# Block products of Strassen type for gates and projection, and conversion of the weights in pieces of 1024 values

## The chip, the cores and the metric

The kernel runs on one core of one Trainium2 chip. Its engines each have a queue of their own: TensorE multiplies matrices (its weight loads are shown apart from its matmuls), VectorE and ScalarE work on tiles element by element, GpSimd does almost nothing here, and SyncE issues all the DMAs. TensorE writes its sums to PSUM; the other tiles lie in SBUF. The metric is the time of one execution on the device in microseconds, and the median of three runs is given.

## The reference

```python
kv = np.einsum('bhsd,bhse->bhde', k, v)          # b 8, h 8, s 576, d 64
out = np.einsum('bhsd,bhde->bhse', q, kv)
rms = np.sqrt(np.mean(out * out, axis=-1, keepdims=True) + 1e-06)
attn = out / rms * g_norm
x = attn.transpose(0, 2, 1, 3).reshape(4608, 512)
h = (x @ w1) * (x @ w2) @ w3                     # w1, w2 512x1024, w3 1024x1024
y = h @ w_out                                    # w_out 1024x512
```

The four weights come as 64-bit floats and are turned into 32-bit ones on the chip. The rest is 32-bit throughout.

## The kernel before

A batch has 576 rows. 512 of them form a group of their own (T = 0 to 7), and the 64 left over of each of the eight batches form the ninth (T = 8), so every group has 512 tokens. For a group the kernel keeps x transposed in `xT[T]` (128 partitions, 4 chunks of the 512 features, 512 tokens).

`gate(T, f)` (line 316) computes block f of 8: two accumulations of four matmuls, weights 128x128 against 512 tokens, one for w1 and one for w2, each in a PSUM bank; ScalarE copies the first to `a_sb`, VectorE multiplies it with the second into `ab[T, f]`. `project(T)` (373) multiplies these blocks with `w3o_sb`, the product of w3 and w_out, which is made once: four output tiles, each an accumulation of eight matmuls 512 wide, then a copy by ScalarE or VectorE and a store.

The stages follow one another. First attention of batch 0 runs. Then the gates of T = 0 run while weights arrive: `load_raw` (115) loads 512 values per partition into a ring of four tiles, and `convert` (121) turns them into 32-bit floats, with two operations on ScalarE and four on VectorE. Then comes the fold: for each of eight blocks of w3 it converts, turns it by TensorE (`turn_w3`, 344) and multiplies it with w_out (`fold_block`, 363). Attention of batch 1 is laid between the fold's blocks. Then follows `project(0)`, and for T = 1 to 8 the gates, with the pieces of attention(T + 1) laid between the blocks, the loads of batch T + 2, and the projection.

`attention(b)` (162) gives pieces for the two halves of the eight heads: `kv`, `q_t`, `product` with its `norm`, and `turn`, which writes `xT`. For odd b it also treats the rows left over of two batches (`q_t_left`, `product_left`, `turn_left`); there are then nine pieces for eight blocks, and the last two follow each other. A piece takes its PSUM banks from `ps_at` (three of them), gates, folds and projections from `ps_mm` (five).

The order on TensorE is that of the program. Up to the end of the gates of T = 0, so are the orders on VectorE, ScalarE and SyncE; from there on a planner orders them. The head of the program, with the order written out:

```python
for name in ("kv1", "q_t01", "q_t11", "turn00", "product01", "turn10"):
    first[name]()
convert_gates(0, raws[0][:1])
first["product11"]()
keep_warm(4)
for name in ("turn01", "turn11"):
    first[name]()
convert_gates(0, raws.pop(0)[1:])
```

## Time and profile before

| | us |
|---|---|
| median of three runs | 956.66 |
| lowest, highest | 955.62, 961.29 |
| the profiled execution | 959.86 |
| its span, first to last instruction | 958.0 |
| TensorE busy | 922.6 |
| VectorE busy | 221.9 |
| ScalarE busy | 189.7 |

The time of an execution holds a little more than the span of its instructions. PE is TensorE, PEld its weight load, DVE VectorE, ACT ScalarE, SPq the queue from which SyncE issues DMAs. A row of a group of instructions gives line, engine, operation, tile written and tiles read, shapes and count, then busy time, the mean duration of one in ns, and the idle time before them with what ended it. A row in order of time gives start, length and the same names; in brackets stands the idle time just before it and what released it. Matmuls overlap, so the length of a row of them is a little more than the time until the next may start; the pace is read from starts. A row of a stretch gives its length, the busy time of PE, PEld, DVE, ACT and POOL with the count of instructions, the clock granted to TensorE (1.00 is full), the busy share of the DMA engines and the GB/s moved.

### The profile page before, as it was taken

The page shows a single profiled execution, that of the slowest core. Times are in us where ns is not written, and L with a number is a line of the kernel's source. Part 1 is how long each engine was busy: PE and PEld are TensorE (multiplying, and loading weights), DVE is VectorE, ACT ScalarE, POOL GpSimd, SP SyncE. Part 2 cuts the span into 40 slices and gives each one's busy share as a digit, 9 for nine tenths or more (in the row PEclk, how much of TensorE's full clock was granted, in tenths as well). Part 3 has the DMA queues.
Part 4 walks back from the last instruction along what each step waited for, and adds up shares of the span by engine and source line. Part 5 has one row for each costly group of instructions (what it writes and reads, how often), then busy time and mean ns, then how long its engine had stood idle before and what let it go on. Part 6 is the DMA issues. An engine that isn't in the chain of part 4 may idle for free.

```text
span 958.0 us, 8045 instructions
## 1 busy us (share of the span) xinstructions
PE 922.6 (96%) x3280; PEld 459.6 (48%) x3280; DVE 221.9 (23%) x421; ACT 189.7 (20%) x364; POOL 0.7 (0%) x6
## 2 busy tenths in 40 slices
PE   7896799999999998999999989999999899999998
PEld 7342455445544554455445544554455444444443
DVE  3878873102110221021102120211021200100010
ACT  3545542102110221022102120221022200000000
POOL 0000000000000000000000000000000000000000
PEclk9898799999999999999999999999999899999999
DMA  8487733002201120022002201220000000000001
GB/s 236 155 267 250 239 99 83 12 33 72 72 11 58 48 72 22 34 72 72 12 34 71 72 12 44 72 61 22 33 1 1 1 36 8 1 22 23 0 1 44
DMA packets 55620, 59.24 MB, mean 62 GB/s; under 512 B 15136, under 2 KB 47904, under 8 KB 55584
## 3 DMA queue, kind: packets, MB, share of 16 engines
q1 hardware_dynamic: 55584, 58.73, 19.9%
q8 instruction: 26, 0.43, 0.2%
q14 instruction: 10, 0.08, 0.0%
HBM read 49.28 MB, written 9.44 MB: 61 GB/s over the span
## 4 chain that ended last, share of the span: by engine, by line
PE 88%; DMA 4%; DVE 3%; ACT 2%; issue 1%; SPq 1%; ACTq 0%; DVEq 0%
PE mm L321 46%; PE mm L378 26%; PE mm L367 6%; DMA raw<-in_moe_w_dram 3%; PE at L176 3%; PE at L239 3%; PE at L198 2%; PE at L271 1%; PE mm L350 1%; DMA v_sb<-in_v_dram 1%; DVE low L138 1%; ACT w_sb L131 1%; DVE inv L218 1%; DVE xn L226 0%; ACT low L130 0%
## 5 line engine op out<-in xcount | busy, mean ns | idle before, releaser
L321 PE MATMUL mm<-xT,w_sb 128*128 128x512 f32 x1024 | 449.9, 594 | 0.7 <-DVE w_sb L142 0.7
L321 PEld LDWEIGHTS mm<-xT,w_sb 128*128 128x128 f32 x1024 | 191.8, 191 | 226.7 <-issue 222.8
L378 PE MATMUL mm<-w3o_sb,ab 128*128 128x512 f32 x576 | 254.3, 603 | 0.0
L378 PEld LDWEIGHTS mm<-w3o_sb,ab 128*128 128x128 f32 x576 | 111.1, 194 | 138.0 <-issue 138.0
L332 DVE TENSOR_TENSOR ab<-a_sb,mm 128x512 f32<-128x512 f32 x72 | 49.5, 687 | 426.8 <-PE mm L321 426.8
L330 ACT COPY a_sb<-mm 128x512 f32<-128x512 f32 x72 | 42.1, 585 | 208.8 <-PE mm L321 208.8
L386 ACT COPY o_sb<-mm 128x512 f32<-128x512 f32 x18 | 10.6, 586 | 248.7 <-PE mm L378 248.7
L367 PE MATMUL mm<-wo_sb,w3T 128*128 128x512 f32 x128 | 56.8, 597 | 0.0
L388 DVE COPY o_sb<-mm 128x512 f32<-128x512 f32 x18 | 12.5, 692 | 184.9 <-PE mm L378 184.9
L321 PE MATMUL mm<-x_left,w_sb 128*128 128x512 f32 x128 | 55.1, 592 | 0.0
L216 ACT ACTIVATE sq<-at 128x512 f32<-128x512 f32 (+1 forms) x40 | 22.1, 552 | 92.1 <-PE at L239 91.0
L239 PEld LDWEIGHTS at<-kv_bd,qT 128*128 128x128 f32 x256 | 32.9, 192 | 12.8 <-issue 11.5
L321 PEld LDWEIGHTS mm<-x_left,w_sb 128*128 128x128 f32 x128 | 24.3, 190 | 30.6 <-issue 30.6
L367 PEld LDWEIGHTS mm<-wo_sb,w3T 128*128 128x128 f32 x128 | 24.0, 193 | 27.1 <-issue 27.1
L130 ACT ACTIVATE low<-raw 128x512 f32<-128x512 uint32 x40 | 27.1, 678 | 42.1 <-DMA raw<-in_moe_w_dram 26.6
L239 PE MATMUL at<-kv_bd,qT 128*128 128x128 f32 x256 | 33.8, 276 | 0.9 <-ACT qT L200 0.9
L218 DVE TENSOR_REDUCE inv<-sq 128x8 f32<-128x512 f32 (+1 forms) x40 | 25.3, 631 | 31.8 <-ACT sq L216 31.8
L275 ACT ACTIVATE xT<-at,g_col 128x512 f32<-128x512 f32 x32 | 21.9, 685 | 47.3 <-PE at L271 47.3
L200 ACT COPY qT<-at 128x512 f32<-128x512 f32 x32 | 18.5, 585 | 64.3 <-PE at L198 64.3
L138 DVE SCALAR_TENSOR_TENSOR low<-raw,low 128x512 uint32<-128x512 uint32 x40 | 27.3, 685 | 1.6 <-ACT low L130 1.5
L226 DVE TENSOR_TENSOR xn<-at,inv 128x512 f32<-128x512 f32 (+1 forms) x40 | 25.5, 638 | 4.0
L271 PE MATMUL at<-ident,xn 128*128 128x128 f32 x128 | 19.8, 278 | 5.3 <-DVE xn L226 4.8
(44 smaller groups left out, 314.5 us busy)
## 6 DMA issues: line engine op xcount, KB each, us to landing
raw<-in_moe_w_dram SPq DMA_DIRECT2D x32, 512.0 KB, 5.2
k_sb<-in_k_dram SPq DMA_DIRECT2D x16, 512.0 KB, 4.4
v_sb<-in_v_dram SPq DMA_DIRECT2D x16, 512.0 KB, 5.5
q_sb<-in_q_dram SPq DMA_DIRECT2D x16, 512.0 KB, 3.9
out_dram<-o_sb SPq DMA_DIRECT2D x32, 256.0 KB, 2.3
raw<-in_moe_w_out_dram SPq DMA_DIRECT2D x8, 512.0 KB, 5.0
kl_sb<-in_k_dram SPq DMA_DIRECT2D x16, 64.0 KB, 4.3
vl_sb<-in_v_dram SPq DMA_DIRECT2D x16, 64.0 KB, 4.8
```

What stands on the lines that cost most here:

```text
L130: nc.scalar.activation(low, lo, AF.Copy, scale=2.0 ** -51, bias=2.0)
L138: nc.vector.scalar_tensor_tensor(out=low_bits, in0=hi, scalar=0x80000000, in1=low_bits, op0=ALU.bitwise_and, op1=ALU.bitwise_or,)
L176: nc.tensor.matmul(kv_ps[e * D:(e + 1) * D, r, :], lhsT=k_sb[:, h, cols] if j < J else kl_sb[:, h, :], rhs=v_sb[:, h, cols] if j < J else ...
L218: nc.vector.tensor_reduce(out=inv, in_=sq[:, cols].rearrange("p (h d) -> p h d", d=D), axis=AX.X, op=ALU.add,)
L226: nc.vector.tensor_tensor(out=dst, in0=o_ps[:, cols].rearrange("p (n m d) -> p n m d", m=m, d=D), in1=inv.rearrange("p (n m) -> p n m", m= ...
L239: nc.tensor.matmul(o_ps[:, h * P:(h + 1) * P], lhsT=qT[i, half][:, h, :], rhs=bd[:, half * HB + h, :], start=True, stop=True,)
L271: nc.tensor.transpose(t_ps[:, r, j, :], st[i, half][:, j, 2 * r:2 * r + 2, :], ident)
L321: nc.tensor.matmul(g_ps, lhsT=w_sb[:, f, c, :], rhs=xT[T][:, c, :], start=(c == 0), stop=(c == NP - 1),)
L330: nc.scalar.copy(a_sb, prods[0])
L332: nc.vector.tensor_mul(ab[T, f], a_sb, prods[1])
L367: nc.tensor.matmul(f_ps, lhsT=t[:, j, :], rhs=wo_sb[:, j, :], start=(j == 0), stop=(j == KF - 1))
L378: nc.tensor.matmul(o_ps, lhsT=ab[T, f][:, m * P:(m + 1) * P], rhs=w3o_sb[:, f, :], start=(f == 0), stop=(f == KF - 1),)
```

## The change

Gates of T = 1 to 8 and all nine projections become products of 2x2 blocks by a scheme of Strassen type, with seven block products where eight stood (`winograd`). For the gates a pair of feature blocks, p and p + 4, is taken at once, the two halves of the 512 features are the inner blocks, and the two halves of the 512 tokens the columns; w1 and w2 go through it together, as the two halves of a PSUM bank. For the projection the inner blocks are pairs of `ab` and `w3o_sb`. Every matmul is now 256 columns wide.

A product goes into a bank; ScalarE copies that partial sum to SBUF (`keep`) while the bank stays as it is, and a later product is added onto it there. Three banks are used per call. VectorE adds a bank and a kept sum (`done`) and, in the gates, multiplies the two halves. The sums of blocks that the scheme needs are made by VectorE: of the weights once (`sum_w`), of `w3o_sb` once (`combine_w3o`), of `ab` for each pair and group (`sum_ab`), of x for each group (`combine_x`). Each writes three new tiles and one block in place.

The gates of T = 0 and the fold keep their matmuls. Weights are loaded and converted in pieces of 1024 values per partition, w1 and w2 of a block in one piece, through a ring of four such pieces, and each conversion issues the next load. The first conversion now follows the whole of attention of batch 0. The fold takes its blocks in the order 0, 4, 1, 5, 2, 6, 3, 7. The input tiles of a half batch have one buffer in place of two, so the second half is loaded after the first has been used, in the middle of a group's gates. The pieces for the rows left over come one place earlier, so that there are eight pieces always; a pair of blocks has two places for them (`between`). Tiles of the first stages are given back, and the sums take their room. A store of the projection holds two of the four output tiles.

```diff
+    N = G // 2
...
-    inp = ctx.enter_context(tc.tile_pool(name="inp", bufs=2))
-    fold = ctx.enter_context(tc.tile_pool(name="fold", bufs=2))
+    inp = ctx.enter_context(tc.tile_pool(name="inp", bufs=1))
...
+    conv = tc.tile_pool(name="conv", bufs=1)
+    early = tc.tile_pool(name="early", bufs=1)
...
+    w_sb = const.tile([P, KF, 2, NP, P], FP32, name="w_sb")
...
+    def load_raw(*srcs):
+        raw = conv_pool.tile([P, 1024], srcs[0].dtype, name="raw", bufs=RAW)
+        n = 1024 // len(srcs)
+        for i, src in enumerate(srcs):
+            nc.sync.dma_start(
+                out=raw[:, i * n:(i + 1) * n].rearrange("p (c m) -> p c m", c=src.shape[1]),
+                in_=src,
+            )
         return raw
...
+        words = raw.bitcast(U32).rearrange("p (n w) -> p n w", w=2)
+        lo, hi = words[:, :, 0], words[:, :, 1]
+        low = conv_pool.tile([P, 1024], FP32, name="low", bufs=2)
...
+    FOLD_ORDER = [i + h * NF for i in range(NF) for h in range(2)]
+    RAW = 4
+    todo = [("w", 0), ("w", 1), ("w", 2)]
+    for f in range(3, KF):
+        todo += [("w", f)] + [("w_out", f // 2 - 1)] * (f % 2)
+    todo += [("w3", i) for i in FOLD_ORDER]
+    todo.insert(-KF + 2, ("w_out", NF - 1))
...
+    raws = []
+    def load_next():
+        if len(raws) == len(todo):
+            return
+        what, i = todo[len(raws)]
...
+    converted = []
+    w3_sb = {}
+    def convert_next(what):
+        n = len(converted)
+        assert todo[n][0] == what
+        i = todo[n][1]
...
+        convert(dst, raws[n])
+        converted.append(n)
+        load_next()
...
-        x = xT[b] = work.tile([P, NP, G], FP32, name="xT")
+        x = xT[b] = work.tile([P, 2, 2, NP // 2, N], FP32, name="xT")
...
+            dst = x[:, half, i].rearrange("p r (j t) -> p r j t", j=2)
+            nc.scalar.activation(dst, t_ps, AF.Copy, scale=g_col)
...
         if b % 2:
-            pieces[6] += [(q_t_left,)]
-            pieces[7] += [(product_left,)]
-            pieces += [[(turn_left,)]]
+            pieces[5] += [(q_t_left,)]
+            pieces[6] += [(product_left,)]
+            pieces[7] += [(turn_left,)]
...
+    ab = [const.tile([P, 4, N], FP32, name=f"ab{p}") for p in range(NF)]
...
-        a_sb = work.tile([P, G], FP32, name="a_sb")
+        a_sb = conv_pool.tile([P, G], FP32, name="a_sb", bufs=2)
         nc.scalar.copy(a_sb, prods[0])
-        ab[T, f] = work.tile([P, G], FP32, name="ab", bufs=KF + 1)
-        nc.vector.tensor_mul(ab[T, f], a_sb, prods[1])
+        half = f // NF
+        nc.vector.tensor_mul(
+            ab[f % NF][:, 2 * half:2 * half + 2, :],
+            a_sb.rearrange("p (i t) -> p i t", i=2),
+            prods[1].rearrange("p (i t) -> p i t", i=2),
+        )
...
+    def winograd(lhsT, rhs, chunks, done, between=lambda: None):
+        def product(a_name, b_name, to=None):
+            ps = to if to is not None else bank(ps_mm, "mm").rearrange("p (u n) -> p u n", u=2)
+            for u in range(2):
+                for c in range(chunks):
+                    nc.tensor.matmul(
+                        ps[:, u, :],
+                        lhsT=lhsT(a_name, u, c),
+                        rhs=rhs(b_name, c),
+                        start=(u == 0 and c == 0 and to is None),
+                        stop=(c == chunks - 1),
+                        skip_group_check=True,
+                    )
+            return ps
+        def keep(name, ps):
+            t = late_pool.tile([P, 2, N], FP32, name=name)
+            nc.scalar.copy(t, ps)
+            return t
+        r1 = product("a11", "b11")
+        p1 = keep("p1", r1)
+        r2 = product("s1", "t1")
+        p5 = keep("p5", r2)
+        product("s2", "t2", r1)
+        u2 = keep("u2", r1)
+        between()
+        product("s4", "b22", r2)
+        done("c12", r2, u2)
+        product("s3", "t3", r1)
+        u3 = keep("u3", r1)
+        done("c22", p5, u3)
+        r3 = product("a12", "b21")
+        done("c11", r3, p1)
+        between()
+        product("a22", "t4", r1)
+        done("c21", r1, None)
+    def combine(b, free):
+        t = {"t1": free[0], "t2": free[1], "t3": b["b12"], "t4": free[2]}
+        args = [
+            (t["t1"], b["b12"], b["b11"]), (t["t2"], b["b22"], t["t1"]),
+            (t["t3"], b["b22"], b["b12"]), (t["t4"], b["b21"], t["t2"]),
+        ]
+        b.update(t)
+        return [lambda a=a: nc.vector.tensor_sub(*a) for a in args]
+    def sums(a, free):
+        s = {"s1": free[0], "s2": free[1], "s3": a["a21"], "s4": free[2]}
+        args = [
+            (s["s2"], s["s1"], a["a11"]), (s["s4"], a["a12"], s["s2"]), (s["s3"], a["a11"], a["a21"]),
+        ]
+        first = (s["s1"], a["a21"], a["a22"])
+        a.update(s)
+        return [lambda: nc.vector.tensor_add(*first)] + [
+            lambda a=a: nc.vector.tensor_sub(*a) for a in args
+        ]
+    def run(*step_lists):
+        for steps in zip(*step_lists):
+            for step in steps:
+                step()
+    xb, wa, aa, ob = {}, {}, {}, {}
+    free = {}
+    def allocate():
+        h = NP // 2
+        for p in range(NF):
+            free["w", p] = late_pool.tile([P, 3, 2, h, P], FP32, name=f"ws{p}")
+        for p in range(NF):
+            free["ab", p] = late_pool.tile([P, 3, N], FP32, name=f"as{p}")
+            free["w3o", p] = late_pool.tile([P, 3, N], FP32, name=f"os{p}")
+    def parts(t):
+        return [t[:, i] for i in range(3)]
+    def combine_x(T):
+        xb[T] = {f"b{i + 1}{j + 1}": xT[T][:, i, j] for i in range(2) for j in range(2)}
+        t = late_pool.tile([P, 3, NP // 2, N], FP32, name="xc")
+        return combine(xb[T], parts(t))
+    def sum_w(p):
+        h = NP // 2
+        wa[p] = {
+            f"a{i + 1}{j + 1}": w_sb[:, p + i * NF, :, j * h:(j + 1) * h]
+            for i in range(2) for j in range(2)
+        }
+        return sums(wa[p], parts(free["w", p]))
+    def sum_ab(p):
+        aa[p] = {name: ab[p][:, i, :] for i, name in enumerate(("a11", "a21", "a12", "a22"))}
+        return sums(aa[p], parts(free["ab", p]))
+    def combine_w3o(p):
+        ob[p] = {
+            f"b{i + 1}{j + 1}": w3o_sb[:, p + i * NF, j * N:(j + 1) * N]
+            for i in range(2) for j in range(2)
+        }
+        return combine(ob[p], parts(free["w3o", p]))
+    AB_OF = {"c11": 0, "c12": 1, "c21": 2, "c22": 3}
+    def gates(T, p, between):
+        def done(name, one, two):
+            dst = ab[p][:, AB_OF[name], :]
+            if two is None:
+                c = late_pool.tile([P, N], FP32, name="c21")
+                nc.scalar.copy(c, one[:, 0, :])
+                nc.vector.tensor_mul(dst, c, one[:, 1, :])
+                return
+            c = late_pool.tile([P, 2, N], FP32, name="c", bufs=2)
+            nc.vector.tensor_add(c, one, two)
+            nc.vector.tensor_mul(dst, c[:, 0, :], c[:, 1, :])
+        winograd(
+            lambda name, w, c: wa[p][name][:, w, c, :],
+            lambda name, c: xb[T][name][:, c, :],
+            NP // 2, done, between,
+        )
+    def project(T, between=lambda: None):
+        o_sb = {}
+        def store(half):
             if T < B:
                 rows = out[T * S:T * S + G, :].rearrange("(p j) f -> p j f", j=J)
-                nc.sync.dma_start(out=rows[:, m, :], in_=o_sb)
+                nc.sync.dma_start(out=rows[:, 2 * half:2 * half + 2, :], in_=o_sb[half])
+                return
+            for m in range(2):
+                for l in range(2):
+                    b = 2 * (2 * half + m) + l
+                    nc.sync.dma_start(
+                        out=out[b * S + G:(b + 1) * S, :], in_=o_sb[half][l * L:(l + 1) * L, m, :]
+                    )
+        def done(name, one, two):
+            half, j = int(name[1]) - 1, int(name[2]) - 1
+            if half not in o_sb:
+                o_sb[half] = late_pool.tile([P, 2, DM], FP32, name="o_sb", bufs=2)
+            dst = o_sb[half][:, :, j * N:(j + 1) * N]
+            if two is None:
+                nc.scalar.copy(dst, one)
             else:
-                for l in range(2):
-                    b = 2 * m + l
-                    nc.sync.dma_start(
-                        out=out[b * S + G:(b + 1) * S, :], in_=o_sb[l * L:(l + 1) * L, :]
-                    )
...
+                nc.vector.tensor_add(dst, one, two)
+            if name in ("c11", "c21"):
+                store(half)
+        winograd(
+            lambda name, m, p: aa[p][name][:, m * P:(m + 1) * P],
+            lambda name, p: ob[p][name],
+            NF, done, between,
+        )
...
-        for name in ("kv1", "q_t01", "q_t11", "turn00", "product01", "turn10"):
+        for name in ("kv1", "q_t01", "q_t11", "turn00", "product01", "turn10", "product11"):
             first[name]()
-        convert_gates(0, raws[0][:1])
-        first["product11"]()
         keep_warm(4)
         for name in ("turn01", "turn11"):
             first[name]()
-        convert_gates(0, raws.pop(0)[1:])
-        convert_gates(1, raws.pop(1))
-        w3_sb = {}
+        early.__exit__(None, None, None)
+        fold_cm = tc.tile_pool(name="fold", bufs=2, reuse_waits="tile")
+        fold = fold_cm.__enter__()
+        for _ in range(2):
+            convert_next("w")
         for f in range(KF):
-            wo_raw = load_wo(f)
-            if f + 2 < KF:
-                raws = load_gates(f + 2)
-                convert_gates(f + 2, raws)
...
-            convert(wo_sb[:, f:f + 1, :], wo_raw)
+            convert_next("w" if f + 2 < KF else "w3")
+            if f % 2:
+                convert_next("w_out")
             gate(0, f)
-            if f in (3, 5):
-                load_half(1, f // 4)
+            if f == 3:
+                load_half(1, 0, inp)
...
-    turn_w3(0, w3_sb.pop(0))
-    for i in range(KF):
-        if i + 2 < KF:
-            w3_sb[i + 2] = convert_w3(load_w3(i + 2))
-        if i + 1 < KF:
-            turn_w3(i + 1, w3_sb.pop(i + 1))
-        pieces[i]()
+    turn_w3(FOLD_ORDER[0])
+    for n, i in enumerate(FOLD_ORDER):
+        if n + 2 < KF:
+            convert_next("w3")
+        if n + 1 < KF:
+            turn_w3(FOLD_ORDER[n + 1])
+        pieces[n]()
+        if n == 1:
+            load_half(1, 1, inp)
         fold_block(i)
-    pieces[KF]()
-    load_batch(2)
+    load_half(2, 0, inp)
+    load_left(2)
+    fold_cm.__exit__(None, None, None)
+    conv.__exit__(None, None, None)
+    late_pool = ctx.enter_context(tc.tile_pool(name="late", bufs=1, reuse_waits="tile"))
+    allocate()
+    run(*(f(p) for p in range(NF) for f in (sum_ab, combine_w3o)))
     project(0)
+    run(sum_w(0), combine_x(1))
+    for p in range(1, NF):
+        run(sum_w(p))
     for T in range(1, NG):
-        pieces = attention(T + 1) if T + 1 < B else []
-        done = 0
-        for f in range(KF):
-            gate(T, f)
-            due = (f + 1) * len(pieces) // KF
-            for piece in pieces[done:due]:
-                piece()
-            done = due
+        pieces = iter(attention(T + 1) if T + 1 < B else [])
+        def between(n=[0]):
+            n[0] += 1
+            next(pieces, lambda: None)()
+            if T + 1 < B and n[0] == 2:
+                load_half(T + 1, 1, inp)
+        for p in range(NF):
+            gates(T, p, between)
+            run(sum_ab(p))
         if T + 2 < B:
-            load_batch(T + 2)
+            load_half(T + 2, 0, inp)
+            load_left(T + 2)
+        if T + 1 < NG:
+            run(combine_x(T + 1))
         project(T)
```

More of the change, by code (lines that the diff above doesn't have):

```diff
@@ L113 @@
     )
-    def load_raw(src):
-        c, n = src.shape[1:]
-        raw = fold.tile([P, c, n], src.dtype, name="raw", bufs=4)
-        nc.sync.dma_start(out=raw, in_=src)
+    def load_raw(*srcs):
[6 more added lines that the diff above has]
+            )
         return raw
@@ L156, with keep_warm @@
     g_col = const.tile([P, 1], FP32, name="g_col")
-    x_left = const.tile([P, NP, G], FP32, name="x_left")
+    x_left = const.tile([P, 2, 2, NP // 2, N], FP32, name="x_left")
     xT = {B: x_left}
+    def keep_warm(n):
+        t = bank(ps_mm, "mm")
+        for _ in range(n):
+            nc.tensor.matmul(t[:, 0:P], lhsT=ident, rhs=ident, start=True, stop=True)
     def attention(b):
@@ L311, in attention @@
         return [steps(fs) for fs in pieces]
-    ab = {}
+    ab = [const.tile([P, 4, N], FP32, name=f"ab{p}") for p in range(NF)]
     def gate(T, f):
         prods = []
-        for w_sb in (w1_sb, w2_sb):
+        for w in range(2):
             g_ps = bank(ps_mm, "mm")
@@ L400, in load_gates @@
-    def load_gates(f):
-        return [(w_sb, load_raw(gate_src(w, f))) for w_sb, w in ((w1_sb, w1), (w2_sb, w2))]
-    def convert_gates(f, raws):
-        for w_sb, raw in raws:
-            convert(w_sb[:, f], raw)
-    def keep_warm(n):
-        t = bank(ps_mm, "mm")
-        for _ in range(n):
-            nc.tensor.matmul(t[:, 0:P], lhsT=ident, rhs=ident, start=True, stop=True)
-    def load_wo(f):
-        return load_raw(w_out[f * P:(f + 1) * P, :].rearrange("p (c f) -> p c f", c=1))
+                nc.sync.dma_start(out=rows[:, 2 * half:2 * half + 2, :], in_=o_sb[half])
@@ L421 @@
     ):
-        for half in range(2):
-            load_half(0, half)
+        early_pool = early.__enter__()
+        load_half(0, 0, inp)
+        load_half(0, 1, early_pool)
         g_src = g_norm.rearrange("(d o) -> d o", o=1)
```

98 lines of the change are left out of this document (37 added, 61 removed).

## The prediction

> **What bounds the kernel now.** I read the page's first part, then the chain that ended last, then the order of time on TensorE.
>
> ```profile
> span 958.0 us, 8045 instructions
> PE 922.6 (96%) x3280; PEld 459.6 (48%) x3280; DVE 221.9 (23%) x421; ACT 189.7 (20%) x364; POOL 0.7 (0%) x6
> PE 88%; DMA 4%; DVE 3%; ACT 2%; issue 1%; SPq 1%; ACTq 0%; DVEq 0%
> ```
>
> TensorE is busy 96% of the span and is 88% of the chain; VectorE and ScalarE have three quarters of the time free. So the sum is a sum over TensorE: what it streams, and where it stands. The chain in order of time gives the pace (start, length, instructions):
>
> ```profile
> 178.89 27.47 PE mm L378 x64
> ...
> 272.17 27.47 PE mm L378 x64
> ...
> 371.04 29.09 PE mm L378 x64
> ...
> 871.04 54.93 PE mm L321 x128
> 925.97 27.48 PE mm L378 x64
> ```
>
> One matmul of the code is two instructions here (a group's gates are 64 matmuls, the row says x128), and 54.93/128 = 429.1 ns is one instruction of 512 columns, with nothing between. A group T costs 54.93 + 27.47 = 82.4 us when alone (T = 7, 8). From the end of one projection to the end of the next (start plus length), T = 1 costs 299.64 - 206.36 = 93.28 with the next batch's attention (10.9), and T = 2, which also carries the rows left over, 400.13 - 299.64 = 100.5.
>
> **Term 1, the products.** Gates of T = 1 to 8: per pair of blocks 7 products of 4 matmuls of 256 columns, so 4 x 7 x 4 x 2 = 224 instructions in place of 128 of twice the width. Projection of T = 0 to 8: 7 x 8 x 2 = 112 in place of 64. In all 1792 + 1008 = 2800 narrow instructions. None of 256 columns is in the trace; the neighbours are 128 and 512:
>
> ```profile
> 114.33 1.04 PE L350 MATMUL mm<-ident,w_sb 128*128 128x128 f32 x8
> 115.21 1.06 PE L239 MATMUL at<-kv_bd,qT 128*128 128x128 f32 x8
> 116.10 0.60 PE L198 MATMUL at<-ident,q_sb 128*128 128x128 f32 x4
> ```
>
> Eight instructions of 128 columns, each with a weight load of its own, start 0.88 to 0.89 us before the next group: 110 to 111 ns each. The weight load is thus hidden at a quarter of the width, and at half has twice the cover. Half of 429.1 is 214.6, twice 110.5 is 221; the line between the two rows gives 216.8. I take 216, near the pure half, as the short groups also pay for switching. Gates 224 x 0.216 = 48.4 (48.1 to 49.5), saving 6.55 a group; projection 112 x 0.216 = 24.2 (24.0 to 24.8), saving 3.27. Total 8 x 6.55 + 9 x 3.27 = 82 us (between 68 and 86).
>
> The Trainium skill's page "TensorE: Matmul & The Clock Gate", section "Back-to-back issue gap", speaks against this: for streams of weight load and matmul it gives about 81 ns at 128 columns and 131 at 512, so that halving the width would keep about three quarters of the cost. The trace has a ratio of 110 to 429 between these widths and does not agree; by the page's ratio the narrow instruction would be an estimated 320 ns.
>
> **Term 2, the added work beside it.** In a pair of gate blocks ScalarE copies four 512-wide sums out of PSUM and one of 256; VectorE makes three 512-wide additions, four 256-wide products and four 256-wide sums (three of 512 in a projection). The nearest rows:
>
> ```profile
> L330 ACT COPY a_sb<-mm 128x512 f32<-128x512 f32 x72 | 42.1, 585 | 208.8 <-PE mm L321 208.8
> L226 DVE TENSOR_TENSOR xn<-at,inv 128x512 f32<-128x512 f32 x32 | 22.1, 692 | 3.1
> L226 DVE TENSOR_TENSOR xn<-at,inv 128x256 f32<-128x256 f32 x8 | 3.4, 425 | 0.8
> 206.50:272.20 65.70, 65.70 (x273) 34.01 (x272) 12.65 (x24) 13.82 (x28) 0.00 (x0) 1.00 0.19 56
> ```
>
> VectorE: 3 x 0.69 + 8 x 0.425 = 5.5 us, ScalarE 4 x 0.585 + 0.4 = 2.7 us, under 12.1 us of TensorE. combine_x (4 x 0.69) lies under the projection. The gates of T = 1 (window row) hold 12.65 us of VectorE and 13.82 of ScalarE; less eight evacuations each (0.69, 0.59), attention adds 7 and 9 us to a group. Neither engine becomes the bound. Uncovered, VectorE's share alone would be 22 us a group.
>
> The latency matters more: the third product goes into the bank of the first, after ScalarE has copied it, with one product (4 matmuls, 1.73 us) in between; the fourth, fifth and seventh likewise. The reaction times:
>
> ```profile
> 299.48 7.03 PE L321 MATMUL mm<-xT,w_sb 128*128 128x512 f32 x16
> 303.11 0.59 ACT L330 COPY a_sb<-mm 128x512 f32<-128x512 f32 x1 [2.80 <-PE mm L321]
> 11.20 1.07 ACT L200 COPY qT<-at 128x512 f32<-128x512 f32 x2
> 11.84 2.05 PE L239 MATMUL at<-kv_bd,qT 128*128 128x128 f32 x16 [0.92 <-ACT qT L200]
> ```
>
> Half of the 16 instructions is done 3.43 us after 299.48, the copy starts 0.2 us later; behind a copy (first of two, 11.20 to about 11.77) TensorE is back in under 0.1. The round trip is 0.2 + 0.59 + 0.1 = 0.9 us against 1.73, and against 3.46 in the projection. So the wait is hidden unless something sits before the copy in ScalarE's queue: attention's square root, which waits for VectorE's reduction, can. I book 0.1 us for each of the 32 pairs, 3 us; the bounds are nothing and 1.5 us a pair (if a 256-wide copy and product, four sums, a reduction and a root, some 3.5 us, stand ahead of the copy, it ends 1.2 us late).
>
> **Term 3, the rows left over.** At T = 2, 4, 6 the last two pieces stand back to back:
>
> ```profile
> 315.56 1.05 PE L239 MATMUL at<-kv_bd,qT 128*128 128x128 f32 x8
> 316.45 0.60 PE L198 MATMUL at<-ident,q_sb 128*128 128x128 f32 x4
> 318.64 0.69 DVE L226 TENSOR_TENSOR xn<-at,inv 128x512 f32<-128x512 f32 x1
> 365.82 1.54 PE L256 MATMUL at<-kv_bd,qT_left 64*64 64x64 f32 x32
> 370.33 0.70 PE L282 MATMUL at<-ident,xn 128*128 128x128 f32 x4 [2.97 <-DVE xn L226]
> ```
>
> Before the last row TensorE stands 2.97 us, and the projection after it takes 29.09 in place of 27.47: 1.6 us of slower matmuls. With product_left one piece earlier, turn_left has three products (5.2 us) before it, and this goes: 4.6 us, three times. What is late next: piece 6 now takes four PSUM banks of the three in ps_at (product, turn, two of product_left). If the fourth gets the first's bank, it waits for that norm; product 315.56 to 316.45 has its xn done at 319.33, 2.9 us on, against 1.2 us of TensorE work: 1.7 us. If it gets the turn's, near nothing. I take 1 us, in the fold stage once too.
>
> The Trainium skill's page "TensorE: Matmul & The Clock Gate", section "The HAM clock gate", puts the drop at an idle window of about 3.4 us; the trace has it after 2.97. By that rule the new stand of 1 to 2 us keeps the clock; if it did not, 3 x 1.6 = 5 us more.
>
> **Term 4, the front.** Now:
>
> ```profile
> 22.86 0.65 ACT L130 ACTIVATE low<-raw 128x512 f32<-128x512 uint32 x1
> 26.23 0.68 DVE L218 TENSOR_REDUCE inv<-sq 128x8 f32<-128x512 f32 x1
> 28.33 1.12 PE L271 MATMUL at<-ident,xn 128*128 128x128 f32 x4 [4.14 <-DVE xn L226]
> 29.24 41.01 PE L321 MATMUL mm<-xT,w_sb 128*128 128x512 f32 x91
> 29.48 0.69 ACT L275 ACTIVATE xT<-at,g_col 128x512 f32<-128x512 f32 x1 [1.67 <-PE at L271]
> 73.12 14.11 PE L321 MATMUL mm<-xT,w_sb 128*128 128x512 f32 x32 [0.72 <-DVE w_sb L142]
> 86.80 0.66 ACT L130 ACTIVATE low<-raw 128x512 f32<-128x512 uint32 x1 [4.99 <-DMA raw<-in_moe_w_dram]
> 90.31 0.66 PE L350 MATMUL mm<-ident,w_sb 128*128 128x128 f32 x4 [3.09 <-DVE w_sb L142]
> 107.00 7.49 PE L367 MATMUL mm<-wo_sb,w3T 128*128 128x512 f32 x16
> 84.00:96.00 12.00, 4.97 (x16) 2.28 (x14) 8.64 (x18) 5.92 (x10) 0.00 (x0) 0.79 0.69 229
> ```
>
> The gates of T = 0 end at 87.2 (90.31 - 3.09); then TensorE waits for w3, and the fold begins at 107.0. Conversions wait for loads (4.99 us at 86.80), because the ring holds 4 x 512 KB. It now holds 4 MB. A conversion of 1024 costs less than two of 512 (VectorE has two operations of 0.42 us, the first of them in the row, and two of 0.685):
>
> ```profile
> L132 DVE TENSOR_SCALAR w_sb<-w_sb 128x512 f32<-128x512 f32 x32 | 13.5, 423 | 13.5 <-ACT w_sb L131 13.0
> L138 DVE SCALAR_TENSOR_TENSOR low<-raw,low 128x512 uint32<-128x512 uint32 x40 | 27.3, 685 | 1.6 <-ACT low L130 1.5
> ```
>
> With 256 wide at 425 and 512 at 692 an element costs 1.04 ns, half of that in the two faster operations, so 2 x 0.69 + 2 x 1.22 = 3.8 us, in place of 4.4. Two gates need three conversions and two products, 12.8 us under 13.7 of TensorE (before: six at 2.2 and two products, 14.7, over it). The ring needs 3 x 1.05 MB in 13.7 us, 230 GB/s, which the window row reaches at 69% of the DMA engines; so the loads stay ahead. Against it: the first conversion, until now split and ahead of the last norm, comes after all of attention(0) and must be whole before gate 0. The norm's square can start at 22.9, where the conversion starts now, its reduction at 23.6 (now 26.23), so the last turn at 25.7, whose ScalarE copy (29.48 now) ends at 27.5; two ScalarE (1.1 each, an estimate from the 0.65) and four VectorE operations of 1024, each begun as the one before allows, take 5.9: gate 0 starts at 33.3, 4.1 later. The gates last 57.3 (57.98 less a wait of 0.7) to 90.6. w3's first two blocks are converted by then, w_out's last at about 92. Two turns (1.8) and piece 0 (2.3) put the first fold at 95, 12 us earlier. The bounds are 92 and 107.
>
> **The sum**, on the span of 958.0: fold start 95; fold to projection 71.9 as now (178.89 - 107.0) plus 1: 168; projection(0) 24.2 plus 1 for its 32 VectorE sums (4 x 8 x 0.425 = 13.6 us, a step of eight under each product of 3.46): 193. T = 1, 3, 5: 93.28 - 9.82 = 83.5 each; T = 2, 4, 6: 100.5 - 9.82 - 4.6 + 1 = 87.1; T = 7, 8: 72.6. Together 657: 850. The tail is 4.55 now, and 5 with four stores behind one copy: 855; bank waits 3: 858. The loads in halves are priced at nothing: half 1 is issued after piece 1 and read in piece 4, some 20 us later, for a landing of 5.5 us:
>
> ```profile
> v_sb<-in_v_dram SPq DMA_DIRECT2D x16, 512.0 KB, 5.5
> ```
>
> Without that cover it is 5.5 us for each of seven batches, 39 in all. The profiled execution took 959.86, its span 958.0, and the median is 956.66; 858 + 1.9 - 3.2 = 857.
>
> **The rivals.** (a) The front gains nothing: VectorE's 12.8 of 13.7 us is a thin cover, or a load is late. Then the fold starts at 107 and the time is 869. (b) The bank waits bind: ScalarE's queue is held by attention in most pairs, 1 to 1.5 us in each of 32: 886 to 902, say 890. For it speaks that square root and copies share an in-order queue; against it that ScalarE is busy some 23 of 83 us. (c) Slower: the narrow matmul costs more than half. The 100 us forecast divided by 2800 is 36 ns, so from 252 ns an instruction it is no gain; at three quarters of 429, 322 ns, it is 857 + 2800 x 0.106 = 1154. Against it: 110 ns at 128 columns. The page named in term 1 gives this ratio.
>
> **Chances.** The forecast 0.67; (a) 0.12; (b) 0.15; (c) 0.04; the mechanism swallowed to within 1%, 0.02. Low end: 214.6 ns (-4), no waits (-5), fold at 92 (-3): 845, taken as 843. High end: into (b), 893. Within 1% of 956.66 is about what a measurement of this kernel can tell from no change (three runs span 955.62 to 961.29). Faster 0.94, same 0.02, slower 0.04. The likeliest alone: 845 to 866.
>
> **What would show it.** 224 and 112 narrow instructions a group at 215 to 217 ns; groups T = 7 and 8 at 72 to 73 us; no idle time of the fold's transposes behind conversion, and a first fold at 92 to 97; TensorE's waits on ScalarE's copies of kept sums near 0; the wait of 2.97 gone and one behind xn at product_left in its place. The forecast is wrong if 256 columns cost over 225 ns, if these waits exceed 0.5 us a pair, or if the fold starts after 100.

## The result, and the profile after

The changed kernel takes 852.72 us (median of 4 runs, 851.15 to 853.81) beside 956.47 for the kernel before on the same chip: a ratio of 0.8903, 95% interval 0.8875 to 0.8931. 857 was predicted, within 843 to 893. The profiled execution took 852.74 us. One of the four executions of run x11 below took 1254.55 us at a granted clock of 0.65, where the others have 0.99, so its figures are those of the other three. First, the page's first part and the shares of the chain that ended last:

```profile
span 850.6 us, 10819 instructions
PE 831.8 (98%) x4480; PEld 683.8 (80%) x4480; DVE 378.3 (44%) x718; ACT 249.2 (29%) x447; POOL 0.7 (0%) x6
PE 96%; DVE 1%; ACT 1%; DMA 1%; issue 0%; SPq 0%; ACTq 0%; DVEq 0%
```

TensorE's busy time fell by 90.8 us (922.6 to 831.8) and its standing by 16.6 (35.4 to 18.8); together the 107.4 that the span lost. VectorE went from 23% to 44% of the span, and its share of the chain from 3% to 1%. The weight loads went from 48% to 80% of the span and have no share in the chain.

Next the chain in order of time (start, length, instructions). The last row of this fence is the end of T = 6, the projections and gates of T = 7 and 8 and all between, without a break:

```profile
32.72 57.99 PE mm L379 x128
94.80 6.87 PE mm L419 x16
...
166.45 29.35 PE mm L432 x136
...
248.12 31.08 PE mm L432 x144
...
334.45 31.08 PE mm L432 x144
...
417.85 31.08 PE mm L432 x144
...
504.17 31.08 PE mm L432 x144
...
673.90 170.96 PE mm L432 x792
```

A narrow instruction is 170.96/792 = 215.9 ns, whether alone or beside attention (31.08/144 = 215.8). From the start of one row of 144 to the next are 86.3 us for T = 2 and T = 4 and 83.4 for T = 3 (a row starts with the last eight instructions of the gates, so this is one group). The rows that took 29.09 and more before, in the projections behind the leftover rows, have no counterpart: all of 144 are equal.

Then the windows (length, PE, PEld, DVE, ACT and POOL busy, granted clock, DMA share, GB/s): the gates of T = 0, the first projection, the last group whole:

```profile
32.72:90.70 57.98, 57.98 (x130) 25.61 (x131) 50.66 (x58) 31.54 (x33) 0.00 (x0) 0.95 0.77 261
166.45:190.60 24.15, 24.15 (x113) 21.26 (x113) 24.08 (x55) 2.35 (x4) 0.00 (x0) 1.00 0.04 17
772.30:844.80 72.50, 72.50 (x337) 63.51 (x335) 22.88 (x47) 13.80 (x25) 0.00 (x0) 1.00 0.04 12
```

In the first projection VectorE makes its 32 sums and the first of those for the gates, is busy for 24.08 of 24.15 us, and TensorE still doesn't stand. Last, TensorE's longest waits by their releaser (us in total, times, longest):

```profile
PE mm L379 <- DVE w_sb L154: 6.6, 1, 6.6
PE at L327 <- DVE xn L282: 1.4, 1, 1.4
```

The first is the wait for the first converted weights. With the second, TensorE stands 8.1 us ahead of gate 0, where it stood 4.14 us before, for xn. No wait of a product (L432) on ScalarE's copies is in the view at all.

**Where 107.4 us of span came from**, before less after: gates of T = 1 to 8, 8 x (54.93 - 48.3) = 53.0; nine projections, 9 x (27.47 - 24.17) = 29.7; the first fold, 107.0 - 94.6 = 12.4 (94.64 by the timeline, as the 107.0 is; the chain has 94.80); the rows left over, 3 x (100.5 - 9.9 - 86.3) = 12.9; less 0.6, a tail 1.2 longer against small gains.

### The profile page after: what moved, and what is told of

Same layout as the page of the kernel before. It is cut to its first block, busy times and chain, and to the rows that moved or that the text cites. A ratio compares the mean times of both kernels' runs of the same rounds, so it can differ in the third digit from the quotient of the medians.

```text
span 850.6 us, 10819 instructions
## 1 busy us (share of the span) xinstructions
PE 831.8 (98%) x4480; PEld 683.8 (80%) x4480; DVE 378.3 (44%) x718; ACT 249.2 (29%) x447; POOL 0.7 (0%) x6
## 4 chain that ended last, share of the span: by engine, by line
PE 96%; DVE 1%; ACT 1%; DMA 1%; issue 0%; SPq 0%; ACTq 0%; DVEq 0%
PE mm L432 71%; PE mm L379 7%; PE mm L419 6%; PE at L295 3%; PE at L232 3%; PE at L254 2%; PE at L327 2%; PE at L312 1%; PE mm L406 1%; DMA v_sb<-in_v_dram 1%; DVE inv L274 0%; DVE xn L282 0%; PE at L264 0%; PE at L336 0%; ACT sq L272 0%
## 5 line engine op out<-in xcount | busy, mean ns | idle before, releaser
L432 PE MATMUL mm<-xT,w_sb 128*128 128x256 f32 x672 | 154.2, 379 | 0.0
L432 PEld LDWEIGHTS mm<-xT,w_sb 128*128 128x128 f32 x672 | 127.7, 190 | 17.4
L432 PE MATMUL mm<-xc,ws 128*128 128x256 f32 x512 | 115.7, 379 | 0.0
L432 PEld LDWEIGHTS mm<-xc,ws 128*128 128x128 f32 x512 | 97.3, 190 | 13.2
L445 ACT COPY u<-mm 128x512 f32<-128x512 f32 x82 | 48.1, 586 | 193.8 <-PE mm L432 193.8
L432 PE MATMUL mm<-w3o_sb,ab 128*128 128x256 f32 x432 | 96.2, 379 | 0.0
L432 PEld LDWEIGHTS mm<-w3o_sb,ab 128*128 128x128 f32 x432 | 82.1, 190 | 11.6 <-issue 0.5
L379 PE MATMUL mm<-xT,w_sb 128*128 128x512 f32 x128 | 58.0, 617 | 6.6 <-DVE w_sb L154 6.6
L432 PE MATMUL mm<-os,as 128*128 128x256 f32 x288 | 63.6, 379 | 0.0
L432 PEld LDWEIGHTS mm<-os,as 128*128 128x128 f32 x288 | 54.7, 190 | 7.4
L432 PE MATMUL mm<-xc,w_sb 128*128 128x256 f32 x256 | 60.5, 379 | 0.0
L432 PE MATMUL mm<-xT,ws 128*128 128x256 f32 x224 | 53.3, 381 | 0.0
L432 PEld LDWEIGHTS mm<-xc,w_sb 128*128 128x128 f32 x256 | 46.8, 190 | 5.4
L432 PEld LDWEIGHTS mm<-xT,ws 128*128 128x128 f32 x224 | 40.7, 190 | 4.7
```

The source lines that it names most:

```text
L379: nc.tensor.matmul(g_ps, lhsT=w_sb[:, f, w, c, :], rhs=xT[T][:, c // 2, :, c % 2, :], start=(c == 0), stop=(c == NP - 1),)
L432: nc.tensor.matmul(ps[:, u, :], lhsT=lhsT(a_name, u, c), rhs=rhs(b_name, c),  start=(u == 0 and c == 0 and to is None), stop=(c == chunks ...
L445: nc.scalar.copy(t, ps)
```

## The experiments

Each is compared with the kernel before on the same chip; ratios are to it, with 95% intervals. "After" is the changed kernel. Where a run is set against after, the difference is that of medians on different chips; worked out from the ratios it can be up to 2 us different.

### Leftover rows back in their old places (x1), and moved alone (x2)

x1 is after with the pieces of the leftover rows where they were; x2 is the kernel before with only this part of the change.

```diff
 # x1, on after
-            pieces[5] += [(q_t_left,)]
-            pieces[6] += [(product_left,)]
-            pieces[7] += [(turn_left,)]
+            pieces[6] += [(q_t_left,)]
+            pieces[7] += [(product_left,)]
+            pieces += [[(turn_left,)]]
...
+    pieces[KF]()
...
+            if n[0] == KF:
+                for piece in pieces:
+                    piece()
```

> The changed kernel with the pieces for the rows left over put back one place (q_t_left in piece 6, product_left in piece 7, turn_left in a ninth piece straight behind piece 7). Theory: their place alone gives 4.35 us in each of T = 2, 4, 6 (100.5 before, 86.3 now, of which 9.8 are products), 13 us in all, by a stand of about 3 us and slower matmuls behind it; so the time is 852.7 + 13 = 866, and three waits of 2.5 to 3 us before turn_left are back. Rival: the stand is gone because the shorter products leave the queues otherwise ordered, and the place is worth nothing: 852 to 855.

> The kernel before with only the pieces for the rows left over moved one place earlier. Theory: 956.5 - 13 = 943, the stand of 2.97 us at T = 2, 4, 6 gone and their projections back to 27.47 us. Rival (a wait of product_left for a PSUM bank takes its place, up to 1.7 us each with slower matmuls behind it): 948 to 956.

x1: 862.76 us (862.12 to 863.93), 0.9007 (0.8991 to 0.9022), 10.0 above after. x2: 945.21 us (944.37 to 946.51), 0.9867 (0.9849 to 0.9885), about 12 below before. x1's waits, and from its chain the rows that hold the projections of T = 2, 4 and 6:

```profile
PE at L336 <- DVE xn L282: 7.9, 3, 2.6
```

```profile
335.60 33.39 PE mm L432 x144
...
509.88 31.08 PE mm L432 x144
...
682.10 172.39 PE mm L432 x792
```

The stand is back three times at 2.6 us. Slower matmuls follow it twice (33.39 for 31.08; 172.39 for 170.96), and not at T = 4; before, all three projections were slow (29.09, 29.17 and 29.68 us for 27.47). The granted clock (after the five engines' busy times) fell in those two cases and not in the other; the windows begin with the end of each stand, to 0.3 us:

```profile
334.50:338.00 3.50, 3.48 (x11) 2.93 (x12) 0.00 (x0) 0.69 (x1) 0.00 (x0) 0.50 0.00 0
509.00:512.00 3.00, 2.74 (x15) 2.52 (x16) 0.46 (x2) 1.04 (x2) 0.00 (x0) 1.00 0.00 0
681.20:685.00 3.80, 3.77 (x12) 3.17 (x13) 0.00 (x0) 0.69 (x1) 0.00 (x0) 0.55 0.01 2
```

So the price of the old place is 7.9 us for the three stands together, and 0 to 2.3 more behind each. In x2 all three are gone, and this is what the moved pieces look like in its timeline and chain:

```profile
356.83 1.92 PE L256 MATMUL at<-kv_bd,qT_left 64*64 64x64 f32 x32
```

```profile
366.69 27.47 PE mm L378 x64
```

1.92 us for 1.54 before is all that the fourth PSUM bank costs: 0.4 us, in after too (326.27, also 1.92).

### Halved instructions without the block products (x3), and block products in the projection alone (x4)

x3 is the kernel before with each 512-wide matmul of gates and projection as two of 256, each with a weight load of its own, and nothing saved. x4 is after with plain gates for T = 1 to 8 and seven products in the projection only; the sums of weights and of x, which only the gates' products need, are left out.

```diff
 # x3, on before (the gates; the projection likewise)
-            for c in range(NP):
-                nc.tensor.matmul(
-                    g_ps,
-                    lhsT=w_sb[:, f, c, :],
-                    rhs=xT[T][:, c, :],
...
+            for u in range(2):
+                for c in range(NP):
+                    nc.tensor.matmul(
+                        g_ps[:, u * 256:(u + 1) * 256],
+                        lhsT=w_sb[:, f, c, :],
+                        rhs=xT[T][:, c, u * 256:(u + 1) * 256],
...
 # x4, on after
-            gates(T, p, between)
+            for f in (p, p + NF):
+                gate(T, f)
+                between()
```

> The kernel before with every matmul of the gates and of the projection done as two of 256 columns, each with its own weight load; same sums, nothing of the scheme of seven products. It has 2 x 1728 = 3456 such instructions. Theory (a narrow instruction is 215.8 ns, half of 429.1 plus 1.2): 956.5 + 3456 x 0.0012 = 961. Rival (width has a price that the changed kernel only hides by its own order): each instruction 5 ns or more dearer, 974 and up.

> The changed kernel with the gates of T = 1 to 8 as plain accumulations of 512 columns, the projections by seven products as they are; sums of weights and of x left out. Theory: the gates' share of the gain is 8 x (54.93 - 48.34) = 53 us, so 852.7 + 53 = 905, with nothing else moved. Rival (part of the products' gain is order, not streaming): away from 905 by more than 5 us.

x3: 963.63 us (962.88 to 963.92), 1.0057 (1.0041 to 1.0072). Its chain for T = 8:

```profile
791.28 55.25 PE mm L322 x256
846.54 27.63 PE mm L381 x128
```

55.25/256 = 215.8 ns: half of 429.1 plus 1.2. Twice the weight loads cost 0.6%. x4: 905.04 us (904.37 to 905.39), 0.9448 (0.9431 to 0.9465). Its chain for the last two projections and the gates between:

```profile
793.55 24.17 PE mm L433 x112
817.72 54.93 PE mm L379 x128
872.65 24.19 PE mm L433 x112
```

It lies 52.3 above after: the gates' share, by 8 x 6.6 = 53.

### Copies that nobody reads (x7, x8)

After, with each kept sum copied out of PSUM once more (x7) or three times more (x8). The extra copies stand between the last product and the kept copy, so the bank comes free later by as much as they put the kept copy back.

```diff
         def keep(name, ps):
+            extra = late_pool.tile([P, 2, N], FP32, name="extra")
+            for _ in range(1):          # x8: 3
+                nc.scalar.copy(extra, ps)
```

> The changed kernel with every copy of a kept sum out of PSUM done twice, the first into a tile that nobody reads. The round trip from a product's end to the reuse of its bank grows from 0.9 us by one pitch of ScalarE copies, about 0.5, to 1.4, under the 1.73 us of the product between. Theory (the wait is hidden, with 0.8 us to spare): 852.7 to 855, no waits of products on ScalarE. Rival (ScalarE is near its limit where attention lies between): 860 and up.

> The same with every copy of a kept sum done four times. The round trip is then 0.2 + 3 x 0.5 + 0.59 + 0.1 = 2.4 us against 1.73 in the gates, 3.46 in the projection. Theory: at T = 7 and 8, where nothing lies between, the reused banks make TensorE wait 1 to 2.5 us a pair of blocks, so that these groups' gates take 52 to 58 us in place of 48.3, the projections stay at 24.2, and the whole is 880 to 920. Rival (something else than the round trip sets the reuse): the gates at T = 8 stay at 48 to 49.

x7: 852.62 us (851.49 to 852.69), 0.8907 (0.8893 to 0.8921): nothing, and again no wait of a product. The kept copy starts 0.48 us behind the extra one (1.7 us behind the first of three in x8, 827.28 to 829.00):

```profile
780.96 0.58 ACT L447 COPY extra<-mm 128x512 f32<-128x512 f32 x1 [2.38 <-PE mm L432]
781.44 0.59 ACT L448 COPY u<-mm 128x512 f32<-128x512 f32 x1
```

x8: 909.24 us (908.84 to 911.45), 0.9506 (0.9489 to 0.9524). TensorE's waits in x8, and from its timeline the products of one pair of gate blocks of T = 8 (the brackets: idle before, releaser):

```profile
PE mm L432 <- ACT p L448: 25.2, 40, 1.0
PE mm L432 <- ACT u L448: 10.3, 25, 0.7
```

```profile
829.65 1.99 PE L432 MATMUL mm<-xc,w_sb 128*128 128x256 f32 x8 [0.73 <-ACT u L448]
...
836.10 1.99 PE L432 MATMUL mm<-xc,ws 128*128 128x256 f32 x8 [1.00 <-ACT p L448]
838.31 1.99 PE L432 MATMUL mm<-x_left,ws 128*128 128x256 f32 x8 [0.22 <-ACT p L448]
840.54 3.72 PE L432 MATMUL mm<-x_left,w_sb 128*128 128x256 f32 x16 [0.24 <-ACT u L448]
844.99 1.99 PE L432 MATMUL mm<-xc,w_sb 128*128 128x256 f32 x8 [0.72 <-ACT u L448]
...
860.06 1.99 PE L432 MATMUL mm<-xc,w_sb 128*128 128x256 f32 x8 [0.73 <-ACT u L448]
```

Here the bank wait of the prediction's rival (b) can be seen, brought about by copies in place of attention's work: from one pair to the next are 844.99 - 829.65 = 15.3 and 860.06 - 844.99 = 15.1 us for 12.1. So the wait exists, the trace shows it when it binds, and the kernel is further from it than the 0.48 us of one more copy. At some 3 us more a pair, x8's eight pairs of T = 7 and 8 make some 24 of the 56.5 that it lies above; to the other 24 pairs, beside attention, some 1.4 each are left.

### The front: ring and size of the conversion (x5, x6, x11)

x5 halves the ring of raw weights (two buffers of 1 MB for four). x6 keeps the ring, and converts each buffer in two passes of 512, as before the change. x11 does both.

```diff
 # x5, x11
-    RAW = 4
+    RAW = 2
 # x6, x11, at the head of convert
+        if dst.shape[1] == 1024:
+            for half in range(2):
+                part = slice(half * 512, (half + 1) * 512)
+                convert(dst[:, part], raw[:, part])
+            return
```

> The changed kernel with a ring of two pieces of 1024 in place of four: 2 MB in flight, as much as before. Theory (the front gains by the deeper ring): a piece is then loaded only after the conversion two before it, some 6 us of issue and landing against 3.7 us of the conversion between, so VectorE waits and the first fold starts 5 to 12 us later than at 94.8: 858 to 865. Rival (the front gains by the cheaper conversion alone): no change, 853.

> The changed kernel with the ring of four pieces of 1024, each converted in two passes of 512. Theory: a conversion costs 4.3 us of VectorE in place of 3.7, so two gates need 3 x 4.3 + 1.3 = 14.2 us under 13.7 of TensorE; the cover is just gone and the first fold starts 2 to 4 us later: 855 to 857. Rival (the front gains by the ring alone): 852 to 853.5. Rival (the gain is all the conversion's): the fold starts at 104 or later, 862 and up.

> The changed kernel with both: a ring of two pieces of 1024, and each converted in two passes of 512, about what the kernel before has. Theory (with 2 MB in flight a load begins only when a conversion has given its room back, so loads and conversions take turns and a conversion's cost counts; with 4 MB it is hidden): 14 conversions before the first fold at 0.53 us more are 7.4 us, less 2.6 for the earlier first gate, so the first fold starts at about 107 (102.7 with the ring alone) and the time is 865 to 869. Rival (the cost of a conversion counts in neither ring): only the earlier first gate is left, fold at 100, 859 to 860.

x5: 862.14 us (861.86 to 862.68), 0.901 (0.8997 to 0.9024). x6: 850.13 us (850.05 to 850.76), 0.8886 (0.8871 to 0.8902), 2.6 *below* after (1.6 by the ratios). x11: 860.53 us (860.27 to 862.59), 0.9004 (0.8965 to 0.9042). x5's waits show the conversion waiting for loads, of which after has none:

```profile
ACT low L142 <- DMA raw<-in_moe_w_dram: 18.0, 8, 4.4
ACT low L142 <- DMA raw<-in_moe_w_out_dram: 15.0, 4, 7.0
```

The timelines at the first gate and the first fold, of after, x5, x6 and x11 in this order:

```profile
32.72 57.99 PE L379 MATMUL mm<-xT,w_sb 128*128 128x512 f32 x128 [6.65 <-DVE w_sb L154]
...
94.64 7.03 PE L419 MATMUL mm<-wo_sb,w3T 128*128 128x512 f32 x16
```

```profile
32.74 58.00 PE L379 MATMUL mm<-xT,w_sb 128*128 128x512 f32 x128 [6.64 <-DVE w_sb L154]
...
102.72 5.56 PE L419 MATMUL mm<-wo_sb,w3T 128*128 128x512 f32 x8
```

```profile
30.09 56.63 PE L384 MATMUL mm<-xT,w_sb 128*128 128x512 f32 x128 [4.13 <-DVE w_sb L159]
...
92.01 7.03 PE L424 MATMUL mm<-wo_sb,w3T 128*128 128x512 f32 x16
```

```profile
30.15 57.33 PE L384 MATMUL mm<-xT,w_sb 128*128 128x512 f32 x128 [4.12 <-DVE w_sb L159]
...
101.74 2.81 PE L424 MATMUL mm<-wo_sb,w3T 128*128 128x512 f32 x5
```

From the start of gate 0 to the first fold are 77.8 us before (107.0 - 29.24), 70.0 in x5, 71.6 in x11, 61.9 in after and in x6. So the ring makes 8 to 10 us of it (70.0 or 71.6 less 61.9). The size of the conversion makes nothing in the ring of four, and in the ring of two 1.6 (71.6 less 70.0), within what single profiles differ by, as x2 shows below. What the size does is to delay gate 0 by 2.6 us, since the first buffer must be whole: the first fold of x6 is 2.6 us earlier too. The expectation of x6, that dearer conversion would hold TensorE up, fell, and that of x11 with it.

Between before and x11 lie 6.2 us (77.8 - 71.6), with the same raw bytes in the ring and the same width of a conversion. How much of this is real is not certain: x2, whose head is that of before, has 75.4 us from gate 0 to the first fold (28.59 to 104.02), and x3, with the loads and conversions of before too, has 77.8. So 3.8 to 6.2 us are to be explained.

### Half of batch 1's inputs out of the weights' way (x12)

The kernel before, with half 1 of batch 1 loaded in the fold stage, as after does, for these 6 us.

```diff
-            if f in (3, 5):
-                load_half(1, f // 4)
+            if f == 3:
+                load_half(1, 0)
...
+        if i == 1:
+            load_half(1, 1)
```

> The kernel before with one thing moved: the second half of batch 1 (1.7 MB) is loaded in the fold stage behind its second piece, as in the changed kernel, and not among the weights. Theory (what the ring and the conversion leave unexplained of the front is this load: 77.8 us from the first gate to the first fold before, 71.6 with ring and conversion as before): at some 270 GB/s the weights behind it come 6 us earlier, the first fold starts at 101 in place of 107.0, and the time is 950 to 951. Rival (the order of the weights' loads does it): the fold stays at 106 to 107, 956 to 957.

955.41 us (10 runs, 951.91 to 959.35), 0.9969 (0.9947 to 0.9991); its first fold comes at 104.68, 75.5 us behind gate 0 (29.21), and x2 has 75.4 without this edit. It is inconclusive, for a reason that SyncE's queue in its timeline shows:

```profile
67.23 0.39 SPq L77 DMA_DIRECT2D k_sb<-in_k_dram  x1
...
77.65 0.43 SPq L77 DMA_DIRECT2D v_sb<-in_v_dram  x1
...
84.70 0.39 SPq L77 DMA_DIRECT2D q_sb<-in_q_dram  x1
```

The second half's loads are still issued among the weights, spread out but not behind them. Their new place lies behind the gates of T = 0, where a planner and not the program orders this queue, and they are issued ahead of that place. In after, where a half's tiles have one buffer, they are issued from 93.99 us on. Whether the 4 to 6 us are these bytes or the order of the weights' loads stays open.

### Two mends (x9, x10)

x9 is after with the first buffer converted in two halves, the first ahead of attention's last product, as before the change. x10 adds that the last group's rows are stored by column halves, each as soon as its sum is there.

```diff
 # x9, x10
-        for name in ("kv1", "q_t01", "q_t11", "turn00", "product01", "turn10", "product11"):
+        for name in ("kv1", "q_t01", "q_t11", "turn00", "product01", "turn10"):
             first[name]()
+        convert_first(0)
+        first["product11"]()
...
-        for _ in range(2):
-            convert_next("w")
+        convert_first(1)
+        convert_next("w")
 # x10
-            if name in ("c11", "c21"):
-                store(half)
+            if T == B or j == 0:
+                store(half, j)
```

> The changed kernel with its first conversion split in two of 512, the first of them ahead of the last norm of attention(0) as it was before. Theory: gate 0 starts at 29.2 in place of 32.7, the gates of T = 0 stay at 58 us and everything behind moves up, since VectorE's conversions (12.6 us for two gates of 13.7) keep ahead: 849.2, ratio to the changed kernel 0.996. Rival: VectorE is the pace at the end of the gates, w_out's last piece and w3's arrive no earlier, and the fold starts where it does: 852 to 853.

> The same, and the stores of T = 8 as two DMAs for a half of the columns, the first half of the columns stored as soon as it is there, in place of four DMAs behind the last copy. Theory: the tail from TensorE's end to the end of the span is 5.7 us now, of which about 1 to 1.5 is the issue of two more DMAs: 848. Rival: landing alone sets the tail: 849, as without it.

x9: 847.63 us (847.41 to 848.77), 0.8853 (0.883 to 0.8877). x10: 846.73 us (845.91 to 847.17), 0.884 (0.8816 to 0.8863), the fastest kernel here. In x9 gate 0 starts at 28.96, 3.8 us earlier than in after, and its gates take 56.79 us for 57.98, at a granted clock of 0.97 in place of 0.95 (window row of x9; after's stands above). In x10, with the same head, they take 57.30 at 0.96, and in x1, with the head of after, 57.15; so how much of this second gain belongs to the edit is not shown.

```profile
28.96:85.75 56.79, 56.79 (x131) 25.05 (x131) 52.58 (x62) 35.80 (x38) 0.00 (x0) 0.97 0.78 266
```

From the start of ScalarE's last copy to the end of the span are 4.6 us in x10 (840.52 to 845.1) and 5.7 in after (844.88 to 850.6):

```profile
840.52 0.58 ACT L584 COPY o_sb<-mm 128x512 f32<-128x512 f32 x1 [6.27 <-PE mm L439]
```

```profile
844.88 0.59 ACT L576 COPY o_sb<-mm 128x512 f32<-128x512 f32 x1 [6.26 <-PE mm L432]
```

## Why the prediction was right

**Term 1, right in mechanism and size.** 216 ns was taken for the narrow instruction, between 214.6 and 221; it is 215.8, alone (x3) and in the products, and 72.6 us for groups T = 7 and 8 came out at 72.5. x4 confirms the gates' share with 52.3. The choice of the pure half (214.6) over the line between the neighbours (216.8) is not decided: 215.8 lies between them, and whether the extra of the 128-wide groups is their switching or the weight load, no run shows. The figures for streams of weight load and matmul in the Trainium skill's page "TensorE: Matmul & The Clock Gate", section "Back-to-back issue gap", from which 320 ns had been estimated, do not hold for these float32 instructions; the measured 215.8 ns decides. Rival (c) falls.

**Term 2, right, with a term too many.** No engine became the bound. The round trip of 0.9 us against 1.73 holds: x7 puts 0.48 more into it and nothing moves, x8 puts 1.7 more and it binds. The 3 us booked for attention's square root ahead of copies were not there: after has no wait of a product on a copy. Rival (b) falls.

**Term 3, right.** 4.6 us, three times, less 1 for the bank was the forecast, 10.8 in all. After gained 12.9, x2 alone about 12, x1 gives 10 back. Of the two ends for the bank the near-nothing one came, 0.4 us. The slower matmuls behind the stand are a matter of the single case: x1 has them twice of three times, at a granted clock of 0.50 and 0.55.

**Term 4, right number, one wrong reason.** Gate 0 was put at 33.3 (32.72 measured), the first fold at 95 (94.6). But the step "Two gates need three conversions and two products, 12.8 us under 13.7 of TensorE (before: six at 2.2 and two products, 14.7, over it)" named cheaper conversion as a cause. x6 goes back to dearer conversions, over the 13.7 by that sum, and from gate 0 to the fold nothing changes. VectorE is busy for 54.82 of the 56.51 us of x6's gates, and TensorE still doesn't wait in them. Two things can account for that, and neither was tested: two gates took not 13.7 but 56.63/4 = 14.2 us in x6, at a granted clock of 0.97, and two buffers are converted ahead of gate 0. The other half of the step, the deeper ring, is what x5 and x11 show, with 8 to 10 of the 12 us. The remainder, 4 to 6 us less the 3.5 by which gate 0 starts later, was not in the working, and is open. That the first fold came within 0.4 us of the forecast is thus in part luck.

**The size.** The span was forecast at 858 and is 850.6. The waits booked and not met make 3.0, three groups at 86.3 for 87.1 make 2.4, the reserve of 1 us each in the fold stage and in the first projection 2.1, the fold 0.4; the tail, 5.7 for 5, takes 0.7 back. On the other side, 3.2 had been taken off since the profiled execution of before lay above its median; after's lies on it. So the span was 7.4 us off, the time only 4.3, and that difference is luck. What was not met was each time a reserve between two ends, and each time the cheap end came.

## What to carry to other kernels

Where TensorE is the bound and its wide instructions can be halved at half the cost, a seven-product scheme gives nearly its whole eighth, as long as each kept sum leaves PSUM within the product that lies between; doubling the copy there is a quick test of how much room is left. A wait for weights at the start of a stage gave way here to a deeper ring and not to cheaper conversion, and the first buffer alone should be cut small, since nothing covers it. A stand of two or three microseconds between dependent pieces is worth a reorder: the move of three lines gave some 12 us without any of the rest.

## What the runs showed that was not expected

- Weight loads at 80% of the span cost next to nothing: 190 ns of load lie under each 215.8 ns of matmul, and twice the loads cost 0.6% (x3). The lines of the costliest groups in after:

```profile
L432 PE MATMUL mm<-xT,w_sb 128*128 128x256 f32 x672 | 154.2, 379 | 0.0
L432 PEld LDWEIGHTS mm<-xT,w_sb 128*128 128x128 f32 x672 | 127.7, 190 | 17.4
```

- Slow matmuls after a stand come and go. After stands of 2.6 us x1 had them twice of three times, 1.4 and 2.3 us each, with the granted clock at about a half for some microseconds. At gate 0 a stand of 6.65 us gave 57.15 to 58.00 us for 128 instructions (after, x1, x4, x5, x7, x8), one of 4.13 gave 56.63 (x6) and 57.33 (x11): the ranges overlap, so the length of the stand alone does not set it.
- A load written later in the source can still be issued early, where a planner orders the queue (x12).
- The same head of the program took 75.4 us in one profile (x2) and 77.8 in another (before) from gate 0 to the first fold: a difference of 2 us there, between single profiles, shows little by itself.
